# Two linear-attention and expert layers on one core: 83 of 96 transpose sets leave TensorE for VectorE and DMAs through DRAM, and every order is written anew

## The chip, the cores and the metric

One NeuronCore of one Trainium2 chip runs the kernel. The metric is device microseconds of one execution. Five engines have queues of their own: TensorE (PE, with its weight loads PEld), VectorE (DVE), ScalarE (ACT), GpSimd (POOL) and SyncE (SP), which here only issues DMAs.

## What is computed

The input is 2048 rows of 576 numbers. Two kinds of layers alternate, each adding to its input, twice each:

```python
x = x + A(layernorm(x), wqkv, wo)
x = x + B(layernorm(x), w_q, k1, k2, u, v)
# A: q, k, v = x @ wqkv in 32 heads of 18
pq, pk = phi(q), phi(k)                  # phi(t) = (t + 1 if t > 0 else exp(t)) + 1e-6
kv, z = sum over rows of pk^T v, of pk
o = (pq @ kv) / (pq . z);  return o @ wo
# B: 32 heads, 64 experts as 8 x 8, one chosen for each head (so its softmax is 1)
e = 8 * argmax(x @ w_q1 @ k1) + argmax(x @ w_q2 @ k2)
return sum over heads of gelu(x . u[e]) * v[e]
```

## The kernel before, in words

The rows are 16 tiles of 128. Products are made with fp32r operands in two parts: a high part (a copy rounded by ScalarE) and a low part (what is left, by a subtraction on VectorE); a product of 576 columns is 28 matmuls (`product`, lines 205 to 214). "Layer 0" and "layer 1" are the two rounds of A and B, and a tile's row of steps is:

- **front** of A: layernorm to `y` (line 183), transpose of `y` (front_T), the products k, v and q (lines 234 to 254), and front_state, which sums kv and z over all tiles in one PSUM bank, `kva`. q is stored in DRAM (`pq_d`). In layer 1 the q product of tiles 0 to 12 is left for later (late_q), and the transposed tile is kept in DRAM for it (front_keep, late_load, `hl_d`).
- A can go on only when all 16 tiles are in `kva`: state_mask, state_sum and state_fold (lines 301 to 349) make the weights `ohi` and `olo` of the next product from it. These two places, one in each layer, split the run into three stages: before the first state_mask, between the two, and after the second.
- **back** of A: back_scale (pq times z, sum of heads, reciprocal, product: `o`), transpose of `o` (back_oT), back_out (28 matmuls, `ppo`), the residual on VectorE.
- **B**: layernorm, transpose of `y` together with the gate weights `cg` of an earlier tile (exp_T), exp_scores (14 matmuls of 512 columns, `pps`), exp_select (some 14 VectorE instructions that find the expert of each head and count the gates, ending in `cg`, line 498), exp_gelu (ScalarE and GpSimd), exp_out (4 matmuls, `po`), a residual.

Three transposes of a 128x640 tile per tile and layer (`f` in front, `o` and `b` in back) are 96 sets. Each set is five TensorE transposes into PSUM, a copy by ScalarE (the high part, line 102) and a subtraction by VectorE that reads PSUM (the low part, line 103), all in `transposed`, lines 190 to 203.

During the first stage the query weights of B are folded with the keys: 64 loads of 288 KB (fold_load), 64 small products (fold_mm). All loads and stores go through SP's queue.

The order of the work is written out by hand and by a program: a loop for the first stage (lines 724 to 749), `step2` for tiles 5 to 12 of the second (lines 670 to 678), and two texts of pieces (`play`, lines 752 to 806). `in_order` (line 142) chains the instructions of TensorE, ScalarE, VectorE and GpSimd in just this order; an engine takes its instructions one by one and waits at each for its inputs.

Of the kernel before, what the change touches and what calls it, by code (L numbers as in the profile page):

```python
# [22 lines left out]
P = 128  # L23
# [12 lines left out]
NB = 5  # L36
# [17 lines left out]
REM, REM_O = 2, 4  # L54


@with_exitstack
def network(ctx, tc, x_in, wqkv, wo, wq_t, k_t, u_t, v2, c_mask, c_mask4, c_ident, c_code, c_code1, c_scale, c_shift, out):
# [20 lines left out]
    nc.gpsimd.memset(mhalf, -0.5)  # L79
    kpad = cp.tile([P, 2, 56], F32, name="kpad")  # L80
# [15 lines left out]
    hl_d = [dr.tile([P, 2, NB, P], F32, name=f"hl_d{t}") for t in range(NT)]  # L96
# [3 lines left out]
    def split(src, hi, lo, eng=nc.vector):  # L100

        nc.scalar.activation(hi, src, AF.Copy)  # L102
        eng.tensor_tensor(lo, src, hi.bitcast(F32), op=ALU.subtract)  # L103

    def split_mixed(src, dst):

        nc.scalar.activation(dst, src, AF.Copy)
        nc.vector.tensor_tensor(dst[64:], src[64:], dst[64:].bitcast(F32), op=ALU.subtract)
# [3 lines left out]
    staged = [0]  # L112

    def stage(name):
        tag = RING[staged[0] % len(RING)]
        staged[0] += 1
        return wk.tile([P, D], F32, tag=tag, name=name, bufs=BUFS[tag])

    def load_weight(src, c0, rem, name):

        tiles = []
        for b, (r, bl) in enumerate(blocks(rem)):
            st = stage(f"{name}st{c0}_{b}")
            cols = slice(c0, c0 + D)
            if b != rem:
                nc.sync.dma_start(st, src[r:r + P, cols])
            else:
                nc.sync.dma_start(st[:64], src[r:r + 64, cols])
                nc.sync.dma_start(st[64:], src[r:r + 64, cols])
            tiles.append(st)  # L130
        return tiles

    def split_weight(tiles, c0, hi, lo, rem, which=range(NB), eng=nc.vector):
        for b in which:
            cols = slice(c0, c0 + D)
            if b != rem:
                split(tiles[b], hi[:, b, cols], lo[:, blocks(rem)[b][1], cols], eng)
            else:
                split_mixed(tiles[b], hi[:, b, cols])
# [16 lines left out]
    def statistics(xt, n, soon=False):  # L156
# [3 lines left out]
        mv = wk.tile([P, 2], F32, tag="mv", name=f"mv{n}")  # L160
        nc.vector.bn_aggr(mv, st.rearrange("p a b -> p (a b)"))  # L161
        rs = wk.tile([P, 2], F32, tag="rs", name=f"rs{n}")
# [6 lines left out]
    def spread(xt, total, n):  # L169

        m = wk.tile([P, 2], F32, tag="mv", name=f"m{n}")
        nc.gpsimd.tensor_scalar(m[:, 0:1], total, -1.0 / D, 1.0, op0=ALU.mult, op1=ALU.mult)
        nc.scalar.activation(junk, xt, AF.Square, bias=m[:, 0:1], accum_out=m[:, 1:2])
        return m

    def layernorm_sum(xt, m, n):
        rs = wk.tile([P, 2], F32, tag="rs", name=f"rs{n}")
        nc.gpsimd.tensor_scalar(rs[:, 0:1], m[:, 1:2], 1.0 / D, EPS_LN, op0=ALU.mult, op1=ALU.add)
        nc.gpsimd.tensor_tensor(rs[:, 0:1], rs[:, 0:1], mhalf, op=ALU.pow)
        nc.gpsimd.tensor_tensor(rs[:, 1:2], m[:, 0:1], rs[:, 0:1], op=ALU.mult)  # L180
# [9 lines left out]
    def transposed(y, n, more=None, tag="t", step=P):  # L190

        todo = [y[:, b * step:b * step + P] for b in range(NB)] if y is not None else []
        todo += [] if more is None else [more]
        w = len(todo) * P
        pt = psum(f"pt{n}")
        for b, x in enumerate(todo):
            nc.tensor.transpose(pt[:, b * P:(b + 1) * P], x, ident)  # L197
        nb = NB if tag == "t" else NB + 1
# [214 lines left out]
    def exp_T(l, t, c):  # L413
# [3 lines left out]
        if y is None and cg is None:  # L417
            return
# [432 lines left out]
```

## Time and profile before

| | |
|---|---|
| median of 3 runs | 756.18 us (755.93 to 757.08) |
| the profiled execution: first to last instruction | 753.7 us |
| median less that span (what lies around it) | 2.5 us |
| TensorE busy | 736.8 us, 98% |
| VectorE, ScalarE, GpSimd busy | 61%, 38%, 26% |
| granted TensorE clock, mean | 0.998 |
| moved by DMA | 79.48 MB, 31.8% of 16 engines' span |

The profiled execution's own time is its span of 753.7 us; no other time of it is given. The profile's times are microseconds from the span's start. "Mean ns" of a group is the duration of one instruction; neighbours on an engine overlap a little, so that the distance of two starts is often shorter. A DMA's time to landing is counted from its issue on SP.

### The profile page before, as it was taken

The numbers are of one execution on the slowest core, as the hardware profiler recorded it, in microseconds if no ns is written. First come the engines' busy times: TensorE is split into PE (matmuls) and PEld (weight loads), VectorE is DVE, ScalarE is ACT, GpSimd is POOL, SyncE is SP. The second block draws the span as 40 slices with busy tenths as digits, with TensorE's granted clock in tenths as the row PEclk, the third lists the DMA queues.
The fourth block names the chain that finished last, engine by engine and source line by source line (L and its number), as shares of the span: only waits on it lengthen the run. The fifth ranks groups of instructions, "written<-read, shape, count | busy, mean of one in ns | idle before, by whom it ended". The sixth has DMA issues, their size and how long they took to land.

```text
span 753.7 us, 13987 instructions
## 1 busy us (share of the span) xinstructions
PE 736.8 (98%) x5356; PEld 693.2 (92%) x5356; DVE 456.8 (61%) x1008; ACT 289.1 (38%) x586; POOL 197.7 (26%) x540
## 2 busy tenths in 40 slices
PE   7999999999999999999999999999999999999996
PEld 5999989999998989999999999999999999999984
DVE  5532342324246887666666665563366789999996
ACT  5422232232333544444444443533234333343443
POOL 2110001000002543333333342230033343534331
PEclk9999999999999999999999999999999999999999
DMA  9736446631111322222232211321733213111201
GB/s 275 245 125 223 157 171 220 218 118 49 48 63 32 110 89 77 98 84 83 92 105 101 83 67 60 111 68 38 206 107 112 85 65 115 48 48 58 70 33 63
DMA packets 52267, 79.48 MB, mean 105 GB/s; under 512 B 5480, under 2 KB 22376, under 8 KB 52200
## 3 DMA queue, kind: packets, MB, share of 16 engines
q1 hardware_dynamic: 52200, 78.59, 31.8%
q8 instruction: 42, 0.69, 0.4%
q14 instruction: 25, 0.20, 0.1%
HBM read 55.01 MB, written 23.56 MB: 104 GB/s over the span
## 4 chain that ended last, share of the span: by engine, by line
PE 81%; DVE 10%; ACT 3%; issue 2%; POOL 2%; DMA 1%; SPq 0%; DVEq 0%; POOLq 0%; ACTq 0%
PE ppk L212 15%; PE ppv L212 15%; PE ppo L402 13%; PE pps L433 12%; PE ppq L212 11%; PE kva L283 4%; PE fold_ps L550 2%; PE ptf L197 2%; PE ptb L197 2%; PE po L517 2%; PE pto L197 2%; PE m L332 1%; DVE tloo L103 1%; DVE o L379 1%; DVE x L391 1%
## 5 line engine op out<-in xcount | busy, mean ns | idle before, releaser
L219 DVE TENSOR_SCALAR ek<-ek 128x576 f32<-128x576 f32 x32 | 14.7, 459 | 81.4 <-ACT ek L218 76.9
L212 PE MATMUL ppk<-whi,thif 128*128 128x288 f32 x320 | 50.4, 301 | 1.6 <-ACT thif L102 1.6
L402 PE MATMUL ppo<-ohi,thio 126*128 126x288 f32 (+1 forms) x320 | 50.9, 301 | 0.8 <-DVE ct L492 0.5
L212 PEld LDWEIGHTS ppk<-whi,thif 128*128 128x128 f32 x320 | 44.2, 188 | 5.6 <-issue 3.3
L163 POOL TENSOR_SCALAR rsf<-mvf 128x1 f32<-128x1 f32 x16 | 3.1, 192 | 175.6 <-DVE mvf L161 175.4
L212 PE MATMUL ppk<-whi,tlof 128*128 128x288 f32 x320 | 48.7, 296 | 0.3 <-DVE tlof L103 0.3
L212 PE MATMUL ppv<-whi,thif 128*128 128x252 f32 x320 | 48.0, 296 | 0.1
L187 ACT ACTIVATE yb<-x,rsb 128x640 f32<-128x640 f32 x32 | 29.5, 923 | 47.9 <-POOL rsb L180 47.9
L212 PE MATMUL ppv<-whi,tlof 128*128 128x252 f32 x320 | 47.6, 295 | 0.0
L219 DVE TENSOR_SCALAR eq<-eq 128x576 f32<-128x576 f32 x32 | 15.8, 493 | 51.7 <-ACT eq L218 51.7
L433 PE MATMUL pps<-shi,thib 128*128 128x512 f32 x160 | 44.4, 407 | 2.0 <-ACT thib L102 2.0
L402 PEld LDWEIGHTS ppo<-ohi,thio 126*128 126x128 f32 (+1 forms) x320 | 44.6, 189 | 1.9 <-issue 0.7
L212 PEld LDWEIGHTS ppk<-whi,tlof 128*128 128x128 f32 x320 | 44.6, 188 | 0.5 <-DVE tlof L103 0.5
L212 PEld LDWEIGHTS ppv<-whi,tlof 128*128 128x128 f32 x320 | 44.6, 188 | 0.0
L212 PEld LDWEIGHTS ppv<-whi,thif 128*128 128x128 f32 x320 | 44.2, 188 | 0.3 <-ACT thif L102 0.3
L438 ACT ACTIVATE s<-pps 128x512 f32<-128x512 f32 x32 | 19.1, 596 | 61.4 <-PE pps L433 61.4
L433 PE MATMUL pps<-shi,tlob 128*128 128x512 f32 x160 | 42.5, 395 | 0.0
L103 DVE TENSOR_TENSOR tlof<-ptf,thif 128x640 fp32r<-128x640 f32 x32 | 26.2, 818 | 24.3 <-ACT thif L102 24.2
L402 PE MATMUL ppo<-ohi,tloo 126*128 126x288 f32 x256 | 40.3, 295 | 0.0
L402 PE MATMUL ppo<-olo,thio 126*128 126x288 f32 x256 | 40.3, 296 | 0.0
L212 PE MATMUL ppk<-wlo,thif 128*128 128x288 f32 x256 | 39.9, 296 | 0.0
L212 PE MATMUL ppq<-whi 128*128 128x288 f32 x260 | 39.6, 299 | 0.1
(156 smaller groups left out, 1778.6 us busy)
## 6 DMA issues: line engine op xcount, KB each, us to landing
fold<-in_wq_t SPq DMA_DIRECT2D x64, 288.0 KB, 4.8
whi<-hl_d SPq DMA_DIRECT2D x26, 320.0 KB, 3.5
pq_d<-eq SPq DMA_DIRECT2D x19, 288.0 KB
pq<-pq_d SPq DMA_DIRECT2D x19, 288.0 KB, 3.3
xf<-in_x SPq DMA_DIRECT2D x16, 288.0 KB, 4.7
x<-in_x SPq DMA_DIRECT2D x16, 288.0 KB, 2.8
x_d<-x SPq DMA_DIRECT2D x16, 288.0 KB, 3.1
x<-x_d SPq DMA_DIRECT2D x16, 288.0 KB, 2.6
```

The costliest lines, as they stand in the source:

```text
L103: eng.tensor_tensor(lo, src, hi.bitcast(F32), op=ALU.subtract)
L187: nc.scalar.activation(y, x2, AF.Identity, scale=rs[:, 0:1], bias=rs[:, 1:2])
L197: nc.tensor.transpose(pt[:, b * P:(b + 1) * P], x, ident)
L212: nc.tensor.matmul(o[:, at:at + c1 - c0], tt[a == "lo"][:, b, :], wb[:, cols + c0:cols + c1], start=(i == 0), stop=(i == len(todo) - 1))
L219: nc.vector.tensor_scalar(e, e, 1.0, EPS, op0=ALU.min, op1=ALU.add)
L283: nc.tensor.matmul(a[:w, c * HC:(c + 1) * HC], vt[:, c * w:(c + 1) * w], fk[:, c * HC:(c + 1) * HC], start=(t == 0 and c == 0), stop=(t == ...
L332: nc.tensor.matmul(m[:c, h * 512:h * 512 + HALF], kvb[:n, b * HC:b * HC + c], wob[l][b][:n, h * HALF:(h + 1) * HALF], start=True, stop=True)
L402: nc.tensor.matmul(p[:, h * 512:h * 512 + HALF], hl[a][:r, b], w[:r, h * HALF:(h + 1) * HALF], start=(i == 0), stop=(i == len(todo) - 1))
L433: nc.tensor.matmul(p[:, :512], hl[a == "lo"][:, b, :], shi[:, b] if w == "hi" else slo[:, blocks(REM)[b][1]], start=(i == 0), stop=(i == l ...
L438: nc.scalar.activation(s[:, NE:], p[:, :512], AF.Copy)
L517: nc.tensor.matmul(p[:, b * 512:b * 512 + HALF], c[i], vmix[:, b * HALF:(b + 1) * HALF], start=(i == 0 and not based), stop=(i == 1))
L550: nc.tensor.matmul(p[32 * j:32 * j + 32, at:at + c1 - c0], kpad[:, ch // 2, 24 - 8 * a:56 - 8 * a], st[:, c0:c1], start=(a == 0), stop=(a ...
```

## The change

- **Transposes.** 13 sets stay on TensorE (`ON_PE`). The other 83 go through the new `turned` and `landed`: VectorE transposes 32x32 blocks into `q` (SBUF), one DMA writes `q` to DRAM (`t_d`), four DMAs read it back as `r` in pieces of 640 bytes, ScalarE makes the high part and VectorE the low part, now both from SBUF. `y`, `q` and `r` share one ring of 6 buffers (`YB`), the parts one of 4 (`TB`).
- **Low parts.** Those of `b` in layer 1 that came through DRAM are subtracted on GpSimd (13 sets); all others stay on VectorE.
- **phi in layer 1.** VectorE's min-and-add (line 219) is left out; ScalarE makes three passes (Relu, Exp, Identity) for its one.
- **Gates.** The integer counts are turned to floats by ScalarE, and the product `cg` is made by GpSimd. `cg` has a transpose of its own (cT), no longer one with `b`.
- **Loads.** The 64 fold loads come singly or by a few between the other pieces, the last 16 behind the first state_mask. The x tiles 0 and 1 come behind `ident` and three weight blocks.
- **Orders.** One text of pieces for the whole program; SP is now chained in its order too.

```diff
+YB, TB = 6, 4
+ON_PE = {('f',0,0),('f',0,1),('o',0,0),('b',0,0),('f',1,0),('o',1,0),('b',1,0),('o',0,1),('b',0,1),('f',1,1),('b',1,1),('f',1,15),('b',1,12)}
+LEAN = {("q", 1), ("k", 1)}
+LO_POOL = {('b',1)}
...
-    def transposed(y, n, more=None, tag="t", step=P):
...
+    def turned(kind, l, t, y, step=P):
+
+        n = f"{kind}{l}_{t}"
+        if (kind, l, t) in ON_PE:
...
+        q = wk.tile([P, NB * P], F32, tag="y", name=f"q{n}", bufs=YB)
+        src = bass.AP(tensor=y.tensor, offset=y.offset, ap=[y.ap[0], [step, NB], [32, 4], [1, 32]])
+        nc.vector.transpose(q.rearrange("p (q b c) -> p b q c", q=4, b=NB), src)
+        yield
+        nc.sync.dma_start(t_d[kind, t], q)
+        yield
+        return (yield from landed(kind, l, t, stationary))
+
+    def landed(kind, l, t, home, who=None):
+
+        n = f"{kind}{l}_{t}"
+        r = wk.tile([P, NB * P], F32, tag="y", name=f"r{n}", bufs=YB)
+        w = 32 * NB
+        for a in range(4):
+            nc.sync.dma_start(r[32 * a:32 * a + 32].rearrange("r (i e) -> r i e", i=4),
+                              t_d[kind, t][:, a * w:(a + 1) * w].rearrange("(i r) e -> r i e", i=4))
+        yield
+        hi, lo = home(n)
+        src = r.rearrange("p (i b c) -> p b i c", i=4, b=NB)
+        h, l4 = (x.rearrange("p b (i c) -> p b i c", i=4) for x in (hi, lo))
+        nc.scalar.activation(h, src, AF.Copy)
+        yield
+        (nc.gpsimd if (who or kind, l) in LO_POOL or (who or kind, l, t) in LO_POOL else nc.vector).tensor_tensor(l4, src, h.bitcast(F32), op=ALU.subtract)
+        return hi, lo
...
-        nc.scalar.activation(e.rearrange("p (b c) -> p b c", b=2), halves(p), AF.Exp)
-        nc.vector.tensor_scalar(e, e, 1.0, EPS, op0=ALU.min, op1=ALU.add)
+        if lean:
+            nc.scalar.activation(e2, halves(p), AF.Relu, scale=-1.0)
+            nc.scalar.activation(e, e, AF.Exp, scale=-1.0)
+            nc.scalar.activation(e, e, AF.Identity, bias=small[:, 0:1])
...
-        nc.vector.tensor_scalar(c2, ct, 63, None, op0=ALU.bitwise_and)
+        nc.vector.tensor_scalar(ct, ct, 63, None, op0=ALU.bitwise_and)
+        nc.scalar.activation(c2, ct, AF.Copy)
...
-        nc.vector.tensor_tensor(cg, g[:, 2:3].to_broadcast([P, 2, NE]), c2.unsqueeze(1).to_broadcast([P, 2, NE]), op=ALU.mult)
+        nc.gpsimd.tensor_tensor(cg, g[:, 2:3].to_broadcast([P, 2, NE]), c2.unsqueeze(1).to_broadcast([P, 2, NE]), op=ALU.mult)
...
-    with in_order(*ALL):
+    with in_order(*ALL, ET.SP):
+
+        play("""
+            wu0.2 fi0.0 wk0.0 wu0.14 wk0.1 fi0.0 wk0.3 fi0.0 fl0.0 fl0.1 fi0.0 kl0.0 wk0.4 wf0.0 wk0.0 fl0.2 wk0.2 wk0.0 wk0.1
...
+            cT0.4 po0.2 k1.1 cT0.4 po0.4 oT0.5 num0.7 oT0.7 oT0.5 O0.5 num0.8 po0.2 k1.1 oT0.7 fT1.0 fT1.2 S0.6 bT0.6 num0.8 po0.4
```

**Place 1: SP's queue at the program's start.** `xf` is an x tile, `wst` a staged block of weights, `fold` a fold load. Before:

```order
L589 DMA xf_151<-in_x 128x576
L687 DMA ident<-in_c_ident 128x128
L126 DMA wst_0_155<-in_wqkv 128x576
L126 DMA wst_1_157<-in_wqkv 128x576
L128 DMA wst_2_159<-in_wqkv 64x576
```

Of the change:

```order
L726 DMA ident<-in_c_ident 128x128
L122 DMA wst_0_204<-in_wqkv 128x576
L122 DMA wst_1_221<-in_wqkv 128x576
L122 DMA wst_3_224<-in_wqkv 128x576
L634 DMA xf_227<-in_x 128x576
```

The first x tile moved from the first to the fifth place of the queue.

**Place 2: SP's queue in the back of layer 0**, behind the first state_mask. `t_do` and `t_db` are the DRAM tiles of the `o` and `b` sets, `ro` and `rb` their landings (the second number is the row tile), `x` and `pq` the loads of back. Before:

```order
L354 DMA x_4_2741<-in_x 128x576
L359 DMA pq_5_2889<-pq_d_5_108 128x576
L254 DMA pq_d_14_117<-eq_14_2871 128x576
L354 DMA x_5_2887<-in_x 128x576
L359 DMA pq_6_3058<-pq_d_6_109 128x576
```

Of the change:

```order
L206 DMA t_do_170<-qo_4_2951 128x640
L283 DMA pq_d_11_113<-eq_11_2968 128x576
L216 DMA ro_4_3000<-t_do_170 32x4x160 x4
L206 DMA t_do_169<-qo_3_2997 128x640
L216 DMA ro_3_3055<-t_do_169 32x4x160 x4
L206 DMA t_db_184<-qb_2_3051 128x640
L216 DMA rb_2_3124<-t_db_184 32x4x160 x4
L390 DMA x_5_3172<-in_x 128x576
L395 DMA pq_5_3174<-pq_d_5_107 128x576
L206 DMA t_do_172<-qo_6_3136 128x640
L206 DMA t_db_186<-qb_4_3196 128x640
L216 DMA ro_6_3212<-t_do_172 32x4x160 x4
```

A write to DRAM and the four reads that wait for it now follow one another in the queue, set after set, with a load or none between.

**Place 3: TensorE at the program's end.** `pps` are score products, `po` the products of exp_out, `pc` a transpose of `cg`; the number is the row tile. Of both, rows between these are left out; each score product is three rows. Before:

```order
L433 MATMUL pps_14_8915<-shi,tlob_14_8905 128x512 x5
L517 MATMUL po_12_8947<-vmix,thib_14_8904 128x288 x2
L197 MATMUL ptb_15_8959<-ident,yb_15_8956 128x128 x5
L433 MATMUL pps_15_8984<-shi,tlob_15_8967 128x512 x5
L517 MATMUL po_13_8981<-vmix,thib_15_8966 128x288 x2
```

Of the change:

```order
L474 MATMUL pps_10_9064<-shi,tlob_10_9041 128x512 x5
L474 MATMUL pps_15_9093<-shi,tlob_15_9085 128x512 x5
L474 MATMUL pps_11_9178<-shi,tlob_11_9173 128x512 x5
L474 MATMUL pps_12_9281<-shi,tlob_12_9160 128x512 x5
L474 MATMUL pps_8_9302<-shi,tlob_8_9271 128x512 x5
L474 MATMUL pps_9_9357<-shi,tlob_9_9062 128x512 x5
L560 MATMUL po_9_9503<-vmix,chi_9_9499 128x288 x2
```

Six score products, of tiles 10, 15, 11, 12, 8 and 9, now stand behind the last back_out product; two (tiles 14 and 15) stood there before. On VectorE the six selections follow them in the same order.

## Rows read from the trace of the kernel before

**Rows 1.** The page: span, and its part 1 (busy us, share, instructions).

```profile
span 753.7 us, 13987 instructions
...
PE 736.8 (98%) x5356; PEld 693.2 (92%) x5356; DVE 456.8 (61%) x1008; ACT 289.1 (38%) x586; POOL 197.7 (26%) x540
```

**Rows 2.** Windows by stage: PE, PEld, DVE, ACT, POOL busy (instructions), PEclk, DMA share, GB/s.

```profile
535.90:753.70 217.80, 207.87 (x1374) 192.29 (x1373) 178.19 (x406) 82.72 (x157) 79.06 (x208) 0.99 0.24 76
228.70:535.90 307.20, 304.28 (x2163) 290.31 (x2164) 196.24 (x438) 132.58 (x269) 97.67 (x272) 1.00 0.27 88
0.00:228.70 228.70, 224.61 (x1820) 210.62 (x1820) 82.42 (x165) 73.82 (x160) 20.94 (x60) 1.00 0.47 158
```

**Rows 3.** Timeline of TensorE in the second stage: start, us, what.

```profile
409.71 0.71 PE L197 MATMUL ptf<-ident,yf 128*128 128x128 f32 x5
410.26 1.05 PE L283 MATMUL kva<-ek,v 128*127 128x126 f32 x8
...
411.27 0.71 PE L197 MATMUL pto<-ident,o 128*128 128x128 f32 x5
411.77 1.43 PE L433 MATMUL pps<-shi,thib 128*128 128x512 f32 x5
...
415.14 0.43 PE L517 MATMUL po<-vmix,thib 128*128 128x288 f32 x2
```

**Rows 4.** Groups by form on VectorE, ScalarE, GpSimd: busy us, mean ns, idle before.

```profile
L103 DVE TENSOR_TENSOR tlof<-ptf,thif 128x640 fp32r<-128x640 f32 x32 | 26.2, 818 | 24.3 <-ACT thif L102 24.2
...
L391 DVE SCALAR_TENSOR_TENSOR x<-ppo,x 128x576 f32<-128x576 f32 x32 | 24.1, 752 | 7.3 <-PE ppo L402 7.0 <-POOL rsf L180 0.2
...
L219 DVE TENSOR_SCALAR eq<-eq 128x576 f32<-128x576 f32 x32 | 15.8, 493 | 51.7 <-ACT eq L218 51.7
L379 DVE TENSOR_TENSOR o<-pq,r 128x576 f32<-128x576 f32 x19 | 15.4, 812 | 0.7
...
L218 ACT ACTIVATE eq<-ppq 128x576 f32<-128x576 f32 x32 | 20.6, 648 | 44.5 <-PE ppq L212 41.8 <-issue 2.6
...
L103 POOL TENSOR_TENSOR wlo<-wst,whi 128x576 fp32r<-128x576 f32 x1 | 1.4, 1426 | 4.5 <-ACT whi L102 4.5
```

**Rows 5.** DMA issues: out<-in, count, KB each, median us to landing.

```profile
whi<-hl_d SPq DMA_DIRECT2D x26, 320.0 KB, 3.5
...
hl_d<-tlof SPq DMA_DIRECT2D x13, 320.0 KB, 3.2
```

**Rows 6.** Tile `hl_d`: SP's issue time ns min/median/max; landing of its reads.

```profile
L267 SPq DMA_DIRECT2D whi<-hl_d x13: 359/370/878, 526.2 to 628.8; - x13
...
DMA to landing us min/median/max: 2.5/3.5/5.3
```

**Rows 7.** Timeline of the start: SP's first issues.

```profile
0.74 0.39 SPq L589 DMA_DIRECT2D xf<-in_x  x1
...
1.18 0.42 SPq L687 DMA_DIRECT2D ident<-in_c_ident  x1
...
1.65 0.90 SPq L126 DMA_DIRECT2D wst<-in_wqkv  x2
```

**Rows 8.** Window of the first back tiles of layer 0 (columns as rows 2).

```profile
250.00:300.00 50.00, 49.07 (x329) 45.54 (x327) 41.49 (x95) 23.04 (x49) 20.77 (x58) 1.00 0.27 92
```

**Rows 9.** The chain that ended last, its end: start us, us, what.

```profile
726.88 0.53 PE po L517 x4
...
732.70 3.55 PE pps L433 x14
...
736.27 0.61 ACT s L438
...
742.85 0.34 DVE mt L461
...
744.50 0.20 DVE tlob L103
...
747.83 0.30 DVE cg L498
```

More of the change, by code (lines that the diff above doesn't have):

```diff
@@ L79, in network @@
     nc.gpsimd.memset(mhalf, -0.5)
+    small = cp.tile([P, 1], F32, name="small")
+    nc.gpsimd.memset(small, EPS)
     kpad = cp.tile([P, 2, 56], F32, name="kpad")
@@ L133, in split_weight, with weight @@
[L133 to L139, printed above, removed]
+    def weight(c, b):
+        r, bl = blocks(REM)[b]
+        cols = slice((1, 2, 0)[c] * D, (1, 2, 0)[c] * D + D)
+        st = stage(f"wst{c}_{b}", NB * c + b)
+        if b != REM:
+            nc.sync.dma_start(st, wqkv[r:r + P, cols])
+        else:
+            nc.sync.dma_start(st[:64], wqkv[r:r + 64, cols])
+            nc.sync.dma_start(st[64:], wqkv[r:r + 64, cols])
+        yield
+        hi = whi[:, b, cols]
+        nc.scalar.activation(hi, st, AF.Copy)
+        yield
+        if b != REM:
+            (nc.gpsimd if (c, b) == (0, 3) else nc.vector).tensor_tensor(wlo[:, bl, cols], st, hi.bitcast(F32), op=ALU.subtract)
+        else:
+            nc.vector.tensor_tensor(hi[64:], st[64:], hi[64:].bitcast(F32), op=ALU.subtract)
@@ L188, in normalized, with stationary @@
         return y.rearrange("p a b -> p (a b)")
-    def transposed(y, n, more=None, tag="t", step=P):
[L192 to L198, printed above, removed]
-        hi = wk.tile([P, nb, P], F32R, tag=tag + "hi", name=f"thi{n}", bufs=4 if tag == "t" else 1)
-        lo = wk.tile([P, nb, P], F32R, tag=tag + "lo", name=f"tlo{n}", bufs=4 if tag == "t" else 1)
-        yield
-        split(pt[:, :w], hi.rearrange("p a b -> p (a b)")[:, :w], lo.rearrange("p a b -> p (a b)")[:, :w])
+    def stationary(n):
+        return tuple(wk.tile([P, NB, P], F32R, tag=a, name=f"{a}{n}", bufs=TB) for a in ("thi", "tlo"))
@@ L236, in front_k @@
         yield
-        tt["fk", l, t] = phi(k, f"k{l}_{t}")
+        tt["fk", l, t] = yield from phi(k, f"k{l}_{t}", ("k", l) in LEAN)
     def front_v(l, t):
@@ L252, in front_q @@
         yield
-        fq = phi(q, f"q{l}_{t}")
+        fq = yield from phi(q, f"q{l}_{t}", ("q", l) in LEAN)
+        yield
         nc.sync.dma_start(pq_d[l][t], fq)
@@ L262, in late_load, with home @@
     def late_load(l, t):
-        at = (1 + t // 2 % 2) * D + t % 2 * 2 * P
-        hi, lo = whi[:, :, at:at + P], whi[:, :, at + P:at + 2 * P]
-        nc.sync.dma_start(hi.bitcast(F32), hl_d[t][:, 0])
-        nc.sync.dma_start(lo.bitcast(F32), hl_d[t][:, 1])
-        tt["f", l, t] = hi, lo
+        def home(n=None):
+            at = (1 + t // 2 % 2) * D + t % 2 * 2 * P
+            return whi[:, :, at:at + P], whi[:, :, at + P:at + 2 * P]
+        if (l, t) in KEPT:
+            hi, lo = home()
+            nc.sync.dma_start(hi.bitcast(F32), hl_d[t][:, 0])
+            nc.sync.dma_start(lo.bitcast(F32), hl_d[t][:, 1])
+            tt["f", l, t] = hi, lo
+        else:
+            tt["f", l, t] = yield from landed("f", l, t, home, "late")
     def late_q(l, t):
@@ L272, in late_q @@
         yield
-        tt["pq", l, t] = phi(q, f"q{l}_{t}")
+        tt["pq", l, t] = yield from phi(q, f"q{l}_{t}", ("q", l) in LEAN)
     def front_state(l, t):
@@ L657, in network @@
+            for i in range(n[0] if n else 99):
+                if g is None or next(g, begun) is begun:
+                    break
+            else:
+                begun[f, l, t] = g
     fl, ln, lv, sv = first_load, first_ln, load_vu, split_vu
     k, v, q, fT, st = front_k, front_v, front_q, front_T, front_state
-    wl, mk, zs, M = wo_load, state_mask, state_sum, state_fold
-    ld, num, oT, O = back_load, back_scale, back_oT, back_out
-    S, sel, gel, po = exp_scores, exp_select, exp_gelu, exp_out
```

415 lines of the change are left out of this document (209 added, 206 removed).

## The prediction

> **What bounds the kernel now.** I read the page's busy shares first, then the windows by stage, then TensorE's timeline, then the groups of the engines that take over work, then the chain at the end. TensorE is busy 736.8 of 753.7 us [rows 1]: it idles 4.1 us in the first stage (228.70 less 224.61), 2.9 us in the second, 9.9 us in the third [rows 2]. So TensorE is the bound, and any work taken from it counts in full as long as nobody else becomes late. The next engine is VectorE: 82 of 229 us, 196 of 307 and 178 of 218 [rows 2]. The third stage is the one to watch: TensorE is full and VectorE is at 82%. ScalarE (83 of 218) and GpSimd (79 of 218) are far from it.
>
> **What TensorE loses.** A set of five transposes moves the start of the next product by 0.55 us (409.71 to 410.26) or 0.50 us (411.27 to 411.77) [rows 3]; I take 0.53. 83 sets are 44.0 us: 14 in the first stage 7.4, 41 in the second 21.7, 28 in the third 14.8. The products stay as they are. A `cg` transpose was one of six before and is one alone now. This is the whole gain, **-44.0 us**; it is real only where TensorE would have been the bound without these sets.
>
> **What VectorE gets.** No row shows its transpose. Between a 128x640 subtraction of 818 ns and a min-and-add of 128x576 at 493 ns [rows 4] as ends for one pass over such a tile, I take 0.75 us, near the first, because one element in and one out is a pass like a subtraction's; 1.5 us, two passes, is the upper bound for the range. [...]
>
> In the third stage VectorE gets 28 transposes, 21.0 us. It loses 16 min-and-adds, 16 x 0.49 = 7.8, and 13 low parts of `b` to GpSimd, 13 x 0.8 = 10.4, and the product `cg`, 16 x 0.3 = 4.8 (`cg`: [rows 9]): it stays at about 176 us, while TensorE falls from 207.9 to 193.1. In the second stage: 196.2 + 41 x 0.75 less some 12 = 215, against 304.3 - 21.7 = 282.6. So on the whole VectorE still fits, 91% of TensorE's work in the third stage, but not in every stretch.
>
> **Costs with one answer.** ScalarE's two more passes for 32 phis are 64 x 0.65 = 42 us [rows 4]; with 289 us busy before [rows 1] it stays under half of the span, and a phi's PSUM bank is freed some 1.3 us later, which the four PSUM buffers hide. GpSimd gets 13 low parts of 1.43 x 640/576 = 1.6 us [rows 4] and 32 small products: 35 to 40 us on 198. I cost both at nothing; TensorE's products cover them. The fold loads are as many as before.
>
> **The start: +2 us.** The first x tile is issued at 0.74 us now; in the new order it stands behind `ident` (0.42) and three weight blocks (0.45 each) [rows 7], so 1.8 us later, and the first layernorm, transpose and k product with it. Bounds 0 (the weight blocks may be what is late) and 5 (16 DMA engines are shared from the first microsecond).
>
> **The first back tiles of layer 0: +5 us.** In 50 us of that stretch TensorE works 49.1 us and VectorE 41.5 [rows 8]. The order puts seven sets by VectorE there (the second place of the order shows `o` of 4, 3, 6 and `b` of 2, 4; `o` 5 and `b` 3 follow). TensorE falls by 3.7 to 45.4 us, VectorE rises by 5.2 to 46.7. Counted along the written order from the score product of tile 1 to the k product of tile 1 in layer 1, with the prices of these rows, TensorE has about 31 us of products and VectorE 38 to 40. I take 5 of these 7 to 9 us, since VectorE has little to do just ahead. Bounds 0 and 10.
>
> **The way through DRAM: +4 us.** A set took 0.5 us on TensorE, 0.7 on ScalarE and 0.8 on VectorE. Now: transpose 0.75, write 3.2 us to landing, four reads 3.5 us to landing [rows 5] plus three more issues of 0.37 [rows 6], then high and low part 1.5: 10 us. The nearest row for the reads is `whi` from `hl_d`: 320 KB too, in pieces of 512 bytes against 640 here. Counted along the order, with 3.7 us for a product of 28 matmuls and 3.37 for scores (411.77 to 415.14 [rows 3]), TensorE has more than 10 us of work between a set's transpose and its first product in 69 of 83 sets (median 17 us, in the first stage 22 and more). The other 14 lack 36 us in sum, but they stand close together, two or three in flight at once, and eight of them lie in the stretches that are priced above and below. I take 4; bounds 0 and 25.
>
> **The end: +6 us.** At the end of the order (third place), six score products stand behind the last back_out product, where two stood. Each is followed by a selection on VectorE, which takes 4.8 us (742.85 to 747.83, less 0.20 for another row between [rows 9]). So from the end of tile 10's scores: 0.65 for ScalarE's copy, six selections 28.8, other rows between them 2.6, then as before from `cg` to the span's end 5.6 (748.13 to 753.7 [rows 9, 1]) and 0.5 for the longer way of `cg` over ScalarE and GpSimd: 38.2 us. TensorE has 22.1 us of work in them (five scores 16.9, six po's at 0.53 [rows 9] 3.2, small ones 2). It idles 16.1 us, where the whole third stage idled 9.9: +6. Bounds 3, and 12 if VectorE arrives there late.
>
> **Sum.** 753.7 - 44.0 + 2 + 5 + 4 + 6 = 726.7 us of span; the median of the runs is 2.5 us above the profiled span, so 729.2, **729 us**.
>
> [...] A low part that came through DRAM has two SBUF inputs, where before one was PSUM. Rows for 576 columns: 812 ns with two SBUF inputs (line 379), 752 with PSUM (line 391) [rows 4], with GpSimd busy 26% of the time [rows 1]. At 0.06 us each, 70 such low parts are 4 us on an engine that is mostly not the bound; less than 1 in the sum. [...]
>
> **The rivals.**
> - *Nothing but the end is late* (chance 0.18). The orders were made for these latencies and hide start, ramp and DRAM. For it: the median slack of 17 us. Against it: the stretch in which VectorE has more work than TensorE. 753.7 - 44.0 + 6 + 2.5 = 718 us.
> - *VectorE's transpose takes two passes*, 1.5 us (0.14). The third stage has 176 + 21 = 197 us on VectorE against 193 on TensorE plus its idle end: some 8 us more; the ramp gets 5 and the rest of the second stage 5 more. 747 us. [...]
> - *SP's queue becomes the bound, and the kernel is slower* (0.08). SP waits at a read for its write's landing, with all behind it. With little between, as in the second place of the order, a set holds SP for 3.2 + 5 x 0.37 = 5.0 us. The second stage has 41 sets, 205 us, and some 110 other DMAs at 0.35, 38 us, in 285 us: it fits. It decides from 6.0 us per set on, a landing of 4.2 us. With the longest landing of rows 6, 5.3 us, a set holds SP 7.1 us: 329 us in 285, and in the third stage 28 sets and some 70 others 224 in 203: 65 us more, 794 us. For it: 83 x 640 KB, 53 MB more, go through the same queue. Against it: median landings of 3.2 and 3.5 at 88 GB/s [rows 2, 5], and that SP can stand 3 us per set.
>
> **The numbers.** The forecast's own case has 0.60. The range, 713 to 752, goes from below the first rival (a start and an end that cost nothing) past the second; it leaves out the slower rival and little else. A measurement of this kernel can tell 0.2%, 1.5 us, from no change. Faster by more: 0.60 + 0.18 and most of the second rival, 0.88; within 0.2%: 0.03, between the second and the third; slower: 0.09, the third and a little.
>
> **What would show it.** Right: TensorE busy near 693 us; the transposes on VectorE near 0.75 us; VectorE over 90% and TensorE under in the 35 us before the end, with six selections in a row; the first k product some 2 us later. The second rival shows as a transpose row of over 1 us. The third shows as SP waiting for its own writes most of the second stage, and TensorE waiting there for ScalarE's high parts behind landings. The forecast is wrong if TensorE's idle time outside the end is over 30 us, or if the transposes that are gone were hidden, so that TensorE's busy time falls by much less than 44 us.

## The result, and the profile after

The changed kernel takes **767.83 us** (median of 4 runs, 764.92 to 769.57) beside 756.21 us before (755.93 to 757.08): a ratio of 1.0147, 95% interval 1.0125 to 1.0169. It is 11.6 us slower where 27 us faster were forecast. The profiled execution has a span of 767.8 us; its own time is 769.57, the longest of the four, so the two spans differ by 14.1 us where the medians differ by 11.6. The page, to be held against [rows 1]:

```profile
span 767.8 us, 14154 instructions
...
PE 723.3 (94%) x4941; PEld 658.8 (86%) x4941; DVE 492.6 (64%) x1041; ACT 349.0 (45%) x709; POOL 255.5 (33%) x586
```

TensorE lost 13.5 us of work, not 44, and idles 44.5 us instead of 16.9. By stage (columns as [rows 2]) it idles 6.6, 13.2 and 24.7 us, where it was 4.1, 2.9 and 9.9:

```profile
0.00:227.00 227.00, 220.41 (x1637) 196.88 (x1637) 88.00 (x166) 70.96 (x148) 22.53 (x61) 0.99 0.56 178
227.00:539.00 312.00, 298.84 (x2046) 277.29 (x2045) 222.44 (x473) 165.37 (x342) 120.00 (x288) 0.99 0.59 185
539.00:767.80 228.80, 204.08 (x1262) 184.63 (x1261) 182.19 (x403) 112.64 (x219) 113.02 (x237) 0.96 0.52 156
```

TensorE's span, summed from its timeline by kinds of matmul (each counted to the start of the next, or to its end where a gap follows):

| us | before | after | change | forecast |
|---|---|---|---|---|
| transposes, with `cg`'s | 55.6 | 13.6 | -42.0 | -44.0 |
| fold pieces | 16.9 | 33.6 | +16.7 | 0 |
| scores | 106.6 | 112.7 | +6.1 | 0 |
| all other matmuls | 557.7 | 563.4 | +5.7 | 0 |
| idle | 16.9 | 44.5 | +27.6 | +17 |
| span | 753.7 | 767.8 | +14.1 | -27.0 |

So the exchange did what it says: 42 us left TensorE. Three things took them back: the fold pieces, idle time, and matmuls that take longer, in part at a lower clock.

**The fold pieces.** A piece is two matmuls by 32 columns of weights (128*32), twice in the records (x4 is one piece). TensorE's timeline after the change shows runs of one, two and three pieces, and each time the start of the next product:

```profile
49.69 1.18 PE L593 MATMUL fold_ps<-fold,kpad 128*32 128x320 f32 x12
50.80 1.60 PE L234 MATMUL ppv<-whi,thif 128*128 128x252 f32 x10
...
54.73 1.16 PE L593 MATMUL fold_ps<-fold,kpad 128*32 128x320 f32 x4
55.82 1.60 PE L234 MATMUL ppq<-whi,thif 128*128 128x288 f32 x10
...
60.76 1.17 PE L593 MATMUL fold_ps<-fold,kpad 128*32 128x320 f32 x8
61.86 0.40 PE L234 MATMUL ppq<-whi,thif 128*128 128x288 f32 x1
```

Three pieces take 1.11 us (49.69 to 50.80), one takes 1.09, two take 1.10. A run of eight in the kernel before:

```profile
64.78 2.19 PE L550 MATMUL fold_ps<-fold,kpad 128*32 128x320 f32 x32
66.90 1.33 PE L212 MATMUL ppk<-whi,thif 128*128 128x288 f32 x8
```

Eight take 2.12. The pieces m, m+1, m+2, m+3 write four different groups of 32 PSUM rows, and up to four of different groups cost about as much as one: four take 1.13 us (91.18 to 92.31 in the change's trace, 39.13 to 40.26 in run 1) against 1.09. Two of the same group (pieces 50 and 54, at 222.81 us of the change's trace) take 2.06. Before there were 8 runs of 8; now there are 26 runs of 1 to 5, at 1.09 to 3.1 us.

**Idle time.** TensorE's waits, the groups over 2 us:

```profile
PE pc L456 <- POOL cg L541: 13.4, 8, 6.3
PE fold_ps L593 <- DMA fold<-in_wq_t: 5.2, 2, 5.0
PE pps L474 <- ACT thib L222: 3.9, 3, 1.4
PE ppo L441 <- ACT thio L222: 2.9, 3, 1.3
PE po L560 <- DVE x L430: 2.5, 2, 1.8
PE po L560 <- ACT chi L459: 2.2, 5, 0.7
```

Two groups, `thib` and `thio`, are sets that came through DRAM: 6.8 us in six waits. The largest is `cg`, the gates, and within it one wait of 6.26 us, in the stretch of the first back tiles of layer 0. TensorE's rows there, with the wait at the end of a row:

```profile
284.11 0.43 PE L441 MATMUL ppo<-olo,tloo 112*128 112x288 f32 x2
290.80 0.47 PE L456 MATMUL pc<-ident,cg 128*128 128x128 f32 x1 [6.26 <-POOL cg L541]
290.92 2.48 PE L474 MATMUL pps<-shi,thib 128*128 128x512 f32 x5
```

The chain to this wait runs over VectorE, which is busy 5.68 of the 7 us from 283 to 290, where TensorE is busy 1.54. The rest of the selection that ends in this `cg` stands in VectorE's queue behind the transpose of a `b` set, and that transpose had to wait for its input:

```profile
286.15 0.84 DVE L204 STREAM_TRANSPOSE qb<-yb 128x640 f32<-128x640 f32 x1 [1.04 <-ACT yb L182]
```

**The clock.** The five matmuls at 290.92 last 2.48 us; five of the same shape at 271.33 last 1.33. Their granted clock (PEclk, the number before the DMA share) is 0.50 and 0.53 up to 295 us, right behind the wait, and 1.00 from there to 300; the last 90 us have such stretches too, as the last two rows show with 0.91 and 0.88 in the mean. Before, it was 1.00 over 250 to 300 us [rows 8] and 0.99 in the third stage [rows 2].

```profile
290.00:293.00 3.00, 2.21 (x6) 1.82 (x7) 2.73 (x5) 1.11 (x3) 1.32 (x3) 0.50 0.61 151
293.00:295.00 2.00, 2.00 (x6) 1.54 (x6) 1.75 (x3) 0.00 (x0) 0.25 (x2) 0.53 0.11 45
295.00:300.00 5.00, 4.84 (x33) 4.39 (x32) 2.97 (x7) 1.76 (x4) 1.38 (x5) 1.00 0.39 113
...
720.00:740.00 20.00, 15.87 (x65) 11.93 (x65) 14.57 (x35) 10.02 (x24) 13.29 (x25) 0.91 0.41 125
740.00:754.00 14.00, 11.96 (x49) 9.32 (x48) 13.14 (x36) 5.14 (x15) 6.99 (x15) 0.88 0.06 22
```

Of the 11.8 us that scores and other matmuls became longer, this accounts for the scores' 6.1 (the mean granted clock is 0.981, before 0.998): 13.2 us of their time lie in stretches at a granted clock of 0.50, where by the rows above they take nearly twice as long. Of all TensorE's busy time 19.1 us lie there, so the clock cost some 9.6 us at most (an estimate, half of it), and 3.4 of the 19.1 are the first fold piece and transposes. For the 5.7 us of the other matmuls that leaves little more than 1; where the rest of it comes from, the traces do not tell.

### The profile page after: what moved, and what is told of

It is laid out like the page before. It is cut to its first block, busy times and chain, and to the rows that moved or that the text cites. A ratio compares the mean times of both kernels' runs of the same rounds, so it can differ in the third digit from the quotient of the medians.

```text
span 767.8 us, 14154 instructions
## 1 busy us (share of the span) xinstructions
PE 723.3 (94%) x4941; PEld 658.8 (86%) x4941; DVE 492.6 (64%) x1041; ACT 349.0 (45%) x709; POOL 255.5 (33%) x586
## 4 chain that ended last, share of the span: by engine, by line
PE 62%; DVE 14%; POOL 7%; ACT 6%; issue 4%; DMA 4%; SPq 2%; POOLq 0%; ACTq 0%; DVEq 0%
PE ppq L234 13%; PE ppk L234 13%; PE ppv L234 12%; PE pps L474 7%; PE ppo L441 6%; PE fold_ps L593 4%; PE kva L318 3%; SPq L216 2%; PE po L560 1%; POOL o L407 1%; DMA fold<-in_wq_t 1%; DVE m L508 1%; DVE pi L529 1%; ACT junk L169 1%; DVE o L416 1%
## 5 line engine op out<-in xcount | busy, mean ns | idle before, releaser
L407 POOL TENSOR_TENSOR o<-pq,zb 128x576 f32<-128x576 f32 x19 | 27.7, 1459 | 105.5 <-ACT zb L352 96.7
L474 PE MATMUL pps<-shi,thib 128*128 128x512 f32 x160 | 47.0, 427 | 6.7 <-ACT thib L222 3.9
L274 ACT ACTIVATE v<-ppv 128x252 f32<-128x252 f32 x64 | 21.2, 378 | 51.3 <-PE ppv L234 43.8
L250 DVE SCALAR_TENSOR_TENSOR ek<-ppk,ek 128x576 f32<-128x576 f32 x32 | 24.2, 756 | 28.6 <-ACT ek L244 26.9
L474 PEld LDWEIGHTS pps<-shi,thib 128*128 128x128 f32 x160 | 30.4, 202 | 13.3 <-ACT thib L222 4.6
L593 PE MATMUL fold_ps<-fold,kpad 128*32 128x320 f32 (+1 forms) x256 | 35.4, 416 | 5.2 <-DMA fold<-in_wq_t 5.2
L234 PE MATMUL ppv<-wlo,thif 128*128 128x252 f32 (+1 forms) x256 | 39.3, 295 | 0.0
```

The source lines that it names most:

```text
L234: nc.tensor.matmul(o[:, at:at + c1 - c0], tt[a == "lo"][:, b, :], wb[:, cols + c0:cols + c1], start=(i == 0), stop=(i == len(todo) - 1))
L250: nc.vector.scalar_tensor_tensor(e2, halves(p), 0.0, e2, op0=ALU.max, op1=ALU.add)
L274: nc.scalar.activation(vt[:, c * w:(c + 2) * w].rearrange("p (c e) -> p c e", c=2)[:, :, :HC], x.rearrange("p (c e) -> p c e", c=2), AF.Copy)
L407: nc.gpsimd.tensor_tensor(o[:, :D], pq, zb, op=ALU.mult)
L474: nc.tensor.matmul(p[:, :512], hl[a == "lo"][:, b, :], shi[:, b] if w == "hi" else slo[:, blocks(REM)[b][1]], start=(i == 0), stop=(i == l ...
L593: nc.tensor.matmul(p[32 * j:32 * j + 32, at:at + c1 - c0], kpad[:, ch // 2, 24 - 8 * a:56 - 8 * a], st[:, c0:c1], start=(a == 0), stop=(a ...
```

## The experiments

**1. The fold pieces in fours.** In the text of the order, all 64 pieces (F) are put together by four, as here:

```diff
-fT0.4 fl0.6 F0.2 q0.0 F0.3 st0.1 fT0.4 q0.0 F0.4 q0.1 ln0.7x2 fT0.2 F0.6 F0.1 F0.5 q0.1 wf0.11
+fT0.4 fl0.6 q0.0 st0.1 fT0.4 q0.0 q0.1 ln0.7x2 fT0.2 F0.0 F0.1 F0.2 F0.3 wf0.10 q0.1 wf0.11
```

> The changed kernel with one edit: the 64 fold pieces, which now stand on TensorE in 26 runs of 1 to 5, stand in 16 runs of 4, each at the place of its last piece; the fold loads follow where a buffer needs it. Theory (a piece alone costs about as much as four together: in the trace of the change runs of 1, 2 and 3 pieces lasted 1.07, 1.10 and 1.11 us to the next start, and before a run of 8 lasted 2.12): the fold rows fall from 33.6 us of TensorE to about 17, and the time falls by 14 to 18 us, to 750 to 754. Rival 1 (the fold's time is only where TensorE would wait anyway for the sets through DRAM or for VectorE): the fold rows fall as far, TensorE's idle time grows by as much, and the time stays within 4 us of 767.8. Rival 2 (each piece has a price of its own, 0.5 us): the fold rows stay near 33 us and so does the time.

760.93 us, ratio to before 1.0056 (1.0038 to 1.0073): 6.9 us better than the change, about half of what was expected. A run of four costs 1.13 us, and the fold rows fell by 13.6 us, to 20.0:

```profile
39.13 1.20 PE L593 MATMUL fold_ps<-fold,kpad 128*32 128x320 f32 x16
40.26 1.60 PE L234 MATMUL ppk<-whi,thif 128*128 128x288 f32 x10
```

The price is as the theory has it. The time falls by less, in part because TensorE idles 3.1 us more: a wait of 3.2 us for the loads of the output weights is new, and the wait at the start stays under another name, 4.1 us for the first `y` instead of 5.0 for a fold load. The spans differ by 9.3 us, more than the medians, since the change's profiled execution was its slowest.

**2. The reverse, in the kernel before.** Its runs of eight are cut into runs of two:

```diff
...
-                run(0, (q, t), (fT, t + 1), (st, t))
+                for i, (f, u) in enumerate(((v, t), (q, t), (fT, t + 1), (st, t))):
+                    run(0, (f, u))
+                    fold_mm(groups[2 * i])
+                    fold_mm(groups[2 * i + 1])
...
-            for m in groups:
-                fold_mm(m)
```

> The kernel before with one edit: the 8 runs of 8 fold pieces are cut into 32 runs of 2, one behind each v product, q product, transpose set and state of the same tile. Theory (a run of 2 costs 1.10 us as after the change, and 8 together 2.12 as before): the fold rows rise from 17 to about 35 us, and the time by 16 to 21 us, to 772 to 777. Rival 1 (the small groups are not what costs, but the loads or the work around them in the changed order): the time rises by under 4 us. Rival 2 (a piece alone has a price of 0.27 us, as in the runs of 8): no change within 0.3%.

781.32 us, ratio 1.0335 (1.0321 to 1.0348): 25 us slower, where the theory had 16 to 21. The fold rows rose by 18.5 us, from 16.9 to 35.4, TensorE's idle time by 3.7, and the rest lies in the matmuls behind. Here a run of two:

```profile
45.16 1.17 PE L550 MATMUL fold_ps<-fold,kpad 128*32 128x320 f32 x8
46.26 1.60 PE L212 MATMUL ppq<-whi,thif 128*128 128x288 f32 x10
```

Nothing of the change is in this kernel, so this cause is shown: grouping alone costs what the account of the change shows, and more.

**3. `cg` on VectorE again.**

```diff
...
-        c2 = wk.tile([P, NE], F32, tag="c2", name="c2" + n)
-        nc.scalar.activation(c2, ct, AF.Copy)
...
-        nc.gpsimd.tensor_tensor(cg, g[:, 2:3].to_broadcast([P, 2, NE]), c2.unsqueeze(1).to_broadcast([P, 2, NE]), op=ALU.mult)
+        nc.vector.tensor_tensor(cg, g[:, 2:3].to_broadcast([P, 2, NE]), c2.unsqueeze(1).to_broadcast([P, 2, NE]), op=ALU.mult)
```

> The changed kernel with one edit: the gate product cg is on VectorE again, from integers, without the conversion on ScalarE; the order is the same. Theory (TensorE stands at cg's transpose because cg is in GpSimd's queue behind o products of 1.45 us and low parts of 1.62: 13.4 us of TensorE's waits in the trace): these waits fall to under 4 us, and with them one drop of the granted clock (283.3 to 290.1 us of the span), so the time falls by 8 to 14 us. Rival (VectorE is what is late, and cg only shows it; 32 products of 0.3 us come on top there): the waits move to other results of VectorE, and the time is within 4 us of 767.8 or above.

768.83 us (ratio 1.0151). TensorE still waits 14.3 us for `cg`, now from VectorE, 6.1 at the same place. The theory falls and its rival fits: the gates' move to GpSimd costs nothing that can be measured.

**4 and 5. The sets of `b` on TensorE again**, 27 of the 83, first where the set had landed, then one step earlier (`back` is this case):

```diff
+        back = (kind, l, t) not in ON_PE and kind=="b"
...
-        if (kind, l, t) in ON_PE:
+        if back or (kind, l, t) in ON_PE:
```

> The changed kernel with one edit: the 27 transpose sets of b that go through VectorE and DRAM are made on TensorE, at the place where ScalarE would take the landed set. Theory (a set on TensorE costs 0.53 us of a TensorE that is the bound, and the way through DRAM is rarely late): TensorE's busy time rises by some 14 us, VectorE's falls by 27 x 0.83 less 13 low parts that come back from GpSimd, and the time rises by 5 to 14 us, less where TensorE's waits for b and VectorE go. Rival (the way through DRAM and VectorE's load are what makes the change slow): TensorE's idle time falls by more than 14 us, and the time falls below 764.

> The changed kernel with one edit: the 27 sets of b that go through VectorE and DRAM are made on TensorE at the place where the set was read back, the high part where it had landed; in the earlier run of this kind they were made at the landing's place, one step later, and TensorE waited 10.5 us more for the low parts of these very sets. Theory (a set on TensorE costs 0.53 us of a TensorE that is the bound, and the rest of that run's rise was its late place): TensorE's busy time rises by 14 to 19 us, its idle time by under 6, and the time is 778 to 792 us. Rival (the way through DRAM costs as much as it saves): the time is below 771.

800.36 and 806.17 us: the rivals fall, since nothing was won back, but both theories are far off too. TensorE's busy time rose by 19.0 and 26.0 us and its idle time by 12.8 and 12.5, and the second run was to be better than the first. An order made for one place of a set punishes another, so these runs give no price for a set. A kernel with all 96 sets back on TensorE in this order, meant to price the whole exchange there, gave no time: its engines wait for one another without end. What the exchange is worth in the new order was therefore not measured.

**6. Six sets of the first back tiles on TensorE** (the same edit for o of 3, 4, 6 and b of 2, 3, 4 in layer 0).

> The changed kernel with one edit: six sets of the first back tiles of layer 0 (o of tiles 3, 4 and 6, b of tiles 2, 3 and 4) are on TensorE, at the place where they were read back. Theory (in 262 to 291 us of the span VectorE has more work than TensorE, its transposes stand ahead of the selection of tile 1, and TensorE waits 6.3 us for cg): with 4 transposes fewer ahead of it, 3.4 us, the wait falls to 2 to 4 us, the granted clock stays up there, TensorE gets 6 x 0.53 more, and the time is 764 to 768 us, by 0 to 4 us better. Rival 1 (the wait is for the way through DRAM of these sets): the wait falls by more than 5 us and the time to under 763. Rival 2 (GpSimd's queue holds cg): the wait stays at 5.5 us or more and the time rises by the 3.2 us of TensorE.

770.58 us (1.018; 1.0158 to 1.0202). The wait at that place fell to 3.3 us, as the theory has it, but the waits up to 325 us grew from 0.4, 0.8 and 0.3 us in the change to 0.7, 1.6, 1.0 and 1.7, and the time rose by 2.8 us, about the price of the six sets (the two 95% intervals overlap; runs 7 and 8 repeat it more clearly). Half of the theory held, the half that matters did not.

**7 to 9. Fours and the start.** The fold pieces in fours at better places, and `fl0.0`, the first x tile, ahead of the weight blocks; the second run adds the six sets, the third mends two late fold loads and loads all k weights ahead of the second x tile:

```diff
-wu0.2 fi0.0 wk0.0 wu0.14 wk0.1 fi0.0 wk0.3 fi0.0 fl0.0 fl0.1 fi0.0 kl0.0 wk0.4 wf0.0 wk0.0 fl0.2 wk0.2
+fl0.0 wu0.2 fi0.0 wk0.0 wu0.14 wk0.1 fi0.0 wk0.2 wk0.3 wk0.4 fi0.0 fl0.1 fi0.0 ln0.0 ln0.0 wk0.0 ln0.0
```

> The changed kernel with two edits: the fold pieces in 16 runs of 4, each now at the first place at which its four loads are issued long enough ahead, the last ones early enough that the loads of the output weights do not wait for their buffers; and at the start the first x tile is loaded ahead of the weight blocks, with its statistics, transposes and k product ahead of those of the second tile, and no fold piece there. Theory (both are costs of their own that add up): the fold rows fall to 17 to 20 us, the wait of 3.2 us for the output weights that the first fold experiment showed is gone, the first k product starts by 11 us instead of 15.7, and the time is 748 to 755 us. Rival (TensorE's time that is saved in the first stage is lost again where VectorE is late, from 260 us of the span on): the first stage ends 15 us or more earlier than in the trace of the change, but the time stays over 757 us.

> The kernel of the run before this one, with the six sets of the first back tiles of layer 0 on TensorE as well. Theory (three places, three prices): the time is 1 to 5 us below that of the run before, 745 to 753 us, and below that of the kernel before the change. Rival: the sets' 3.2 us on TensorE are paid and nothing is given back; the time is 2 to 4 us above the run before.

> The fold pieces in 16 runs of 4 and the start with the first x tile ahead, as in the run with both, with two things mended that its trace shows: the first and the fifteenth run of four stand later, since TensorE waited 3.6 and 2.7 us there for their loads, and all five weight blocks of k are loaded ahead of the second x tile, since the first k product waited 4.6 us for them. Theory (the prices add up, no other engine takes the time back): 16 runs at 1.13 us, fold rows under 21 us, first v product at 21 to 23 us instead of 23.6, and the time 748 to 753 us. Rival (what TensorE saves before 260 us it waits for VectorE behind it): the time stays within 2 us of 757.9.

757.86, 760.85 and 755.85 us. The first misses its theory, the second fits its rival: the six sets cost 3.0 again. The last is 12.0 us better than the change and level with the kernel before (0.9987; 0.9977 to 0.9998), though short of its 748 to 753: with the fold's price and most of the start gone, TensorE is busy 709.9 of 755.2 us, and 45 us of idle time have taken the whole rest of the gain.

**10 and 11. A product put into the longest wait.** `q0.13`, which the order keeps back, stands ahead of `cg`'s transpose of tile 0; once in the change, once in the last kernel.

```diff
-num0.5 sel0.0x2 cT0.0 bT0.2
+num0.5 sel0.0x2 q0.13 cT0.0 bT0.2
```

> The changed kernel with one edit: the q product of tile 13 of layer 0, which the order keeps back as work for later, stands on TensorE just ahead of cg's transpose of tile 0, where TensorE waits 6.3 us, instead of some 40 us later. Theory (VectorE fills that stretch and TensorE has nothing of its own there, so the wait is room for a product of 3.7 us, and the clock stays up): the wait falls to about 2.5 us, and the time by 3 to 6 us, to 762 to 765. Rival (the whole stretch up to the last tiles runs at VectorE's pace, so the room comes back 40 us later where the product is missing): the wait falls as far, other waits before 330 us of the span grow by as much, and the time stays within 1.5 us of 767.8.

> The kernel of the run before this one, with the q product of tile 13 in TensorE's longest wait as well. Theory: 2 to 6 us below the run before, 744 to 750 us, faster than the kernel before the change. Rival: as for the product alone, within 1.5 us of the run before.

770.94 and 760.42 us: no gain, even 3 to 5 us lost, which neither side had. In run 10 the wait shrank from 6.26 to 2.56 us, with one of 1.81 right behind it. A new one of 4.06 stands 53 us later, some 20 us behind the place from which the product was taken, and the transpose that waits there starts no earlier than in the change (the last row):

```profile
290.06 0.33 PE L456 MATMUL pc<-ident,cg 128*128 128x128 f32 x1 [2.56 <-POOL cg L541]
...
343.52 0.45 PE L456 MATMUL pc<-ident,cg 128*128 128x128 f32 x1 [4.06 <-POOL cg L541]
...
342.64 0.33 PE L456 MATMUL pc<-ident,cg 128*128 128x128 f32 x1 [0.17 <-POOL cg L541]
```

So this stretch has a length that TensorE does not set, and less work on TensorE there is only more idle time.

**12 to 15. What sets that length?** VectorE's transposes are left out (the write takes the set as it is); reads come from one buffer written once, so that they wait for no landing; the first with `cg` on VectorE; both with pq loaded ahead of x.

```diff
-        nc.vector.transpose(q.rearrange("p (q b c) -> p b q c", q=4, b=NB), src)
...
-        nc.sync.dma_start(t_d[kind, t], q)
+        nc.sync.dma_start(t_d[kind, t].rearrange("p (b c) -> p b c", b=NB), src)
```

> The changed kernel with one edit: the 83 sets are written to DRAM as they are, without VectorE's transpose, and read back as before; so the transposes are left out of the computation. VectorE loses 83 x 0.84 us, 70 us, the way through DRAM stays. Theory (VectorE sets the pace between 225 and 340 us and at the end): TensorE's waits for cg fall from 13.4 to under 6 us, its idle time from 44 to under 34, and the time falls by 8 to 18 us, to 750 to 760. Rival (landings or the order, not VectorE's load): the time stays within 4 us of 767.8.

> The changed kernel with one edit: all sets are read back from one DRAM buffer that the first set wrote once; so the values of the sets are left out, all DMAs and their sizes stay, but no read waits for its own write to land. Theory (VectorE sets the pace; a landing of 2 to 3.5 us is rarely what ends last): the time stays within 3 us of 767.8. Rival (the way through DRAM is what is late): TensorE's waits for high and low parts of landed sets and for what stands behind them vanish, and the time falls by more than 6 us.

> The changed kernel without VectorE's 83 transposes (left out of the computation; the sets are written to DRAM as they are) and with cg on VectorE again, so that neither VectorE's load nor GpSimd's queue stands ahead of cg's transpose. Theory (two queues are equally late at TensorE's wait of 6.3 us): the waits for cg fall from 13 to under 6 us, and the time by 6 to 14 us against the run without the transposes (775.3), to 761 to 769. Rival (TensorE's own order and the length of the way from scores to cg hold the stretch): the waits for cg stay over 10 us, and the time stays within 4 us of 775.3.

> The changed kernel with three edits: VectorE's 83 transposes and the values of the landed sets are left out (sets are written to DRAM as they are, all are read back from one buffer that the first set wrote, so no read waits for its write), and a back tile's pq load is issued ahead of its x load. Theory (several queues are equally late at TensorE's longest wait: VectorE's selection, GpSimd's o that waits for pq, SP's reads that wait for writes): the wait of 6.3 us for cg falls to under 3, TensorE's waits for cg from 13.4 to under 8 in sum, and the time to 752 to 762. Rival (TensorE's own order and the length of the way from scores to cg): the wait stays over 4.5 us, and the time stays over 764.

775.31, 764.76, 776.04 and 772.09 us. Taking 60 us of work from VectorE (busy 432.1 instead of 492.6) made the kernel slower, which neither side had, so VectorE's load alone is not the answer. Without any wait for landings it gains 3.1 us, near the forecast's 4 us for DRAM, though the two 95% intervals overlap. In the run without transposes, the wait for `cg` is 4.5 us, and GpSimd holds the gates: `cg` stands in its queue behind an `o` that waits for its pq load:

```profile
287.32 1.40 POOL L405 TENSOR_TENSOR o<-pq,zb 128x576 f32<-128x576 f32 x1 [2.08 <-DMA pq<-pq_d]
288.67 0.46 POOL L539 TENSOR_TENSOR cg<-g,c 128x128 f32<-128x128 f32 x1
```

In the change itself the same `o` ends at 288.43, only 1.9 us ahead of `cg`. In the run without transposes its load was late on SP behind the reads of a landed set, which had themselves waited:

```profile
280.60 2.74 SPq L214 DMA_DIRECT2D rb<-t_db  x4
283.45 0.37 SPq L388 DMA_DIRECT2D x<-in_x  x1
284.17 0.34 SPq L393 DMA_DIRECT2D pq<-pq_d  x1
```

With `cg` on VectorE as well, VectorE waits at that `o`'s sum, ahead of `cg` in its own queue, and TensorE's waits for `cg` are 12.1 us, as the rival has it. With three queues relieved at once the wait is 3.2 us, but the waits for `cg` are 10.5 in sum and the time is 772. Neither the theory (752 to 762) nor its rival (a wait over 4.5) fits. Several in-order queues are late together at this place; for the end of the kernel, where TensorE idles 19.6 of the last 87.8 us, no run found one cause. The three runs without transposes also hold `y` and `o` until the write has read them, which the change does not, and in the first of them the writes of `f` and `b` take 2.6 and 2.7 us to landing (median) instead of 2.1, so their times are no clean price of a transpose. What sets the length of these stretches stays open.

**16. One more fold load mended** in the best version of the change: the last four issued together.

> The kernel with the fold pieces in fours and the mended start, with the loads of the last four fold pieces issued together with those before them; TensorE waited 2.0 us for them there. Theory: that wait goes, and the time falls by 1 to 3 us, to 752 to 755, below the kernel before. Rival (the stretch behind it runs at another engine's pace): within 1 us of 755.9.

755.82 us: the rival holds, no change.

**17 and 18. Ten sets alone, in the kernel before.** The sets of tiles 4 to 13 of the first stage take the new way, begun one tile earlier; order, fold runs and start stay. In the second run the high part stands behind `v`'s copies on ScalarE, and in tiles with fold pieces the low part behind the q product's phi on VectorE. The edit that makes the second of the first, in part:

```diff
-            if t + 1 in VIA:
-                run(0, (fT, t + 1, 1))
...
             run(0, (v, t))
...
+            if t + 1 in VIA:
+                run(0, (fT, t + 1, 1))
```

> The kernel before with one edit: the sets of tiles 4 to 13 of layer 0 in the first stage, ten of 96, go by VectorE's transpose and through DRAM, begun one tile earlier than they are needed; its order, its fold runs of 8 and its start stay. VectorE is busy 82 of 229 us there. Theory (the exchange brings its 0.5 us per set where TensorE is the bound and VectorE has room): TensorE's busy time falls by 10 x 0.53, 5.3 us, no wait comes in its place, and the time is 749.5 to 752.5 us, a ratio of 0.991 to 0.995. Rival (a set through DRAM costs TensorE as much in waits): within 1.5 us of 756.2, or slower.

> The kernel before with the ten sets of the first stage by VectorE and through DRAM, and one thing mended against the run before of this kind: on ScalarE the high part of a landed set stands behind the two copies of v, on VectorE the low part behind the q product's phi, so that nothing waits behind a landing. Theory (the exchange brings its 0.5 us per set where nothing stands behind the landing): the three waits of the state, 4.5 us, go, TensorE's busy time stays 5 us under that of the kernel before, and the time is 750 to 753 us, a ratio of 0.992 to 0.996. Rival (the landing is then late for the k product of the next tile): as much time is waited at ppk, and the time stays within 1.5 us of 756.5.

The first took 756.32 us, no change (0.9989 to 1.0014): 5.5 us of transposes were gone, and TensorE waited for the state, where it had not before (the second row stands in the kernel before too, with the same 3.1 us):

```profile
PE kva L311 <- ACT v L273: 4.4, 3, 2.3
PE ptb L200 <- DVE cg L526: 3.1, 2, 2.3
```

The copies of `v` stood on ScalarE behind a high part that waited for its landing. The second took **751.66 us, ratio 0.9939 (0.9925 to 0.9952)**, the fastest kernel of this study, 4.8 us better for ten sets. Its largest waits:

```profile
PE ptb L200 <- DVE cg L526: 3.2, 2, 2.3
PE pps L461 <- ACT thib L105: 2.0, 3, 0.9
```

The wait of the state is gone, and nothing took its place.

## Why the prediction was wrong, step by step

- **What TensorE loses, -44.0:** right as a term. It measured -42.0, with `cg`'s own transposes at 4.9 us inside. TensorE's busy time as a whole fell by only 13.5 us.
- **"The fold loads are as many as before", among the costs at nothing: this step failed first.** It looked at loads and left out that the order also scatters the matmuls. That cost 16.7 us on TensorE, shown by runs 1 and 2 from both sides.
- **The products stay as they are: wrong by 11.8 us.** They keep their number, but the scores take 6.1 us more, 13.2 us of them at a granted clock of 0.50 behind waits, and the sum had no term for that. This is read from the traces; no run filled the waits without moving work. Most of the other matmuls' 5.7 us stays open.
- **The end, +6:** the mechanism came, its size did not: the third stage idles 14.8 us more, and VectorE was busy 27.0 of the last 35 us, where the prediction had over 90%. The chain that ended last has the selections in a row (each begins with `mt`), 5.4 and 6.1 us apart, not 4.8:

```profile
744.47 0.43 DVE mt L502
...
749.89 0.34 DVE mt L502
...
755.96 0.34 DVE mt L502
...
761.61 0.49 PE pc L456
```

- **The first back tiles, +5:** the stretch is there, one wait of 6.26 us and smaller ones beside it, 10 us in sum. The reason given, more work on VectorE than on TensorE, is what the trace has there, but it is not enough: with work taken from VectorE the wait falls to 3.3 and 4.5 us and the time does not (runs 6 and 12).
- **The start, +2:** too small. The first k product came at 15.68 instead of 9.55 us, 6.1 later, of which one fold piece takes 2.0.
- **The way through DRAM, +4:** near: 6.8 us of waits for landed sets, and 3.1 us gained without the wait for landings. SP as the bound did not come.
- **VectorE's transpose, 0.75 us:** near. It takes 0.83 to 0.84; two passes it is not:

```profile
L204 DVE STREAM_TRANSPOSE qo<-o 128x640 f32<-128x640 f32 x29 | 24.1, 833 | 2.2 <-POOL o L419 2.0
L224 DVE TENSOR_TENSOR tloo<-ro,thio 128x640 fp32r<-128x640 f32 x29 | 26.2, 903 | 7.1 <-ACT thio L222 7.1
```

- **Low parts with two SBUF inputs, 4 us on VectorE:** they take 0.90 (`tloo`) and 0.86 us (`tlof`), where they took 0.82 before [rows 4]; that is 4 us on VectorE over these 56, as the rows had it (the 14 `tlob` take 0.83). Single instructions show more: on the way to the wait of 6.26 us one took 1.50 us beside an `o` of GpSimd at 286.99 to 288.43, where it took 0.49 ten microseconds before:

```profile
277.35 0.49 DVE L525 TENSOR_TENSOR pr<-oh,m 128x512 bf16<-128x512 bf16 x1
...
287.20 1.50 DVE L525 TENSOR_TENSOR pr<-oh,m 128x512 bf16<-128x512 bf16 x1
```

No run shows what made the second one longer.

Without the fold's 16.7, the longer matmuls' 11.8, 10.6 more idle time and 2.0 of transposes, the span would be the forecast's 726.7. The prediction's sentence "any work taken from it counts in full as long as nobody else becomes late" was the frame, and the order made nearly everybody a little late.

## What to carry to other kernels

Here narrow matmuls (32 columns) of up to four different groups of PSUM rows had a price per run, 1.09 to 1.13 us, not per piece: before an order is rewritten, count the runs that stay side by side. Work taken from an engine at 98% is a gain only where the rest of the order has room: ten sets moved alone gave 0.48 us each, 83 moved with every order made anew gave their 42 us back as idle time, longer matmuls and broken groups. And on an in-order engine nothing that is needed soon may stand behind a landing: moving a landed set's high and low parts behind other steps of ScalarE and VectorE decided between no gain and 4.8 us.

## What was not expected of the hardware

One, two, three or four fold pieces of different groups of 32 PSUM rows took 1.09, 1.10, 1.11 and 1.13 us. After a wait of 6.26 us five matmuls took 2.48 us instead of 1.33, at a granted clock of 0.50 (0.981 in the mean of the span); no run shows whether the wait brought it. And a kernel with 60 us less work on VectorE, all else in the same order, was 7.5 us slower; its writes held `y` and `o` longer, and those of `f` and `b` landed later.
